# Block 0's matmul operands made one unit earlier, in an unused weight place, the operand steps spread over five units, and the last slot block in another order

## The chip, the cores and the metric

The kernel runs on one core of a Trainium2 chip. The metric is the device time of one execution in microseconds (us), as the median over several executions. The core's engines each work through an instruction list of their own and wait for each other by semaphores: TensorE (PE, matmuls), VectorE (DVE), ScalarE (ACT), GpSimd (POOL), and SyncE (SP), which here only starts transfers (DMAs). ACT starts some transfers too, in the same list as its arithmetic.

## The reference

Three stages follow each other, each on the output of the one before, all in float32:

```python
x = attention(q, k, v, omega)          # random features, 4 x 576 tokens, 8 heads of 64 -> (2304, 512)
# stage 2: 4 experts, all of them on all tokens
for e in range(4):
    h = np.maximum(x @ w1[e], 0.0)     # 512 -> 1024
    out += p[:, e:e + 1] * (h @ w2[e]) # 1024 -> 512, p from domain_probs
# stage 3: 32 slots, 4 for each of 8 experts
logits = x @ phi
d = softmax over the tokens of logits
slot_input = d.T @ x                   # 32 x 512
slot_out = relu(slot_input @ w1[e]) @ w2[e]
return softmax over the slots of logits @ slot_out
```

## The kernel before

**Stage 2, where most of the time goes.** The 2304 tokens are cut into three blocks (0 to 2) and the 4 experts into two halves of their hidden width, so 8 groups. A unit is one group on one block; units 0 to 23 run group by group, so units 0 to 2 are the first group on blocks 0, 1, 2. Every number is split into a high and a low part, and a matmul piece is three matmuls (high by high, high by low, low by high).

**Products.** Units 0 to 2 multiply the plain operands: `plain1` runs eight products of the first matrix (PE, line L558, into the accumulators X and B). From unit 3 on the first matrix is multiplied with seven products (`product1`, also L558) of sums of operand quarters, after the Strassen-Winograd scheme. The second matrix is always done with seven products (`product2`, L765), one unit late, interleaved with the next unit's first-matrix products. Between the two lie the evacuations: relu and split into high and low (ACT L542 and L607 for the high parts such as s3h, DVE L545 and L611 for the low parts such as s3l, s2l, s4l), DVE L671, L703 and L625 for sums, ACT L635 to L639 for copies of X into u, and L812/L814 for copies v of the second matrix's result, which DVE adds up at L808 and scales into the output x at L745 and L747.

**Operands.** What units 3 and up multiply has to be made from each block's plain operand first. This is done once for each block b, in steps: W, `whole` (DVE: high plus low into one float32 array, for each of 4 quarters `KH[0..3]`; L489, for block 0 L492 with the low parts from a transfer), T, `block_sum` (DVE L497, 4 differences of quarters, in place), S, `block_split` (for each of 4 results I4 to I7: ACT L508 casts the high part into `xh`, DVE L510 subtracts it, and two ticks later two transfers from ACT's list, L513 and L514, store both to `xt` in DRAM, from which later units load them). `xh` has two places. Which step runs at which place of which unit is a table of numbers in `prep_steps`, keyed (unit, step): an even step 2i follows first-matrix product i, an odd one 2i + 1 second-matrix product i.

**Block 0's source.** Its quarters come back from DRAM (`xd`, written at L282) by eight transfers on SP's list (`fetch`, L469 and L470, high parts into `xr`, low parts into `xl`).

**Slots.** The slot stage takes the finished tokens in blocks b of up to 4 tiles of 128: `slot_turn` (transposes tpm, L983, and ACT copies x2t, L984), `slot_logits` (lq, L992), `slot_sum` (lt, L1003, DVE maximum L1011, ACT exp L1015), `slot_back` (transposes dp, L1044), `slot_gather` (acc, L1062, and its DVE update L1068). Most of these run as tasks in the last units. The last block, of 2 tiles, and what is left of the one before run in an order written out at the end of the stage, up to the first matmul of the slot experts (hq, L1202):

```python
slot_logits(n)
slot_back(n - 1)
keep_warm(4)
slot_sum(n)
slot_gather(n - 1)
keep_warm(6)
keep_warm(10)
slot_back(n)
keep_warm(3)
```

`keep_warm(k)` puts k matmuls (L78, named warm) whose result nobody reads.

Of the kernel before, what the change touches and what calls it, by code (L numbers as in the profile page):

```python
# [9 lines left out]
F32 = mybir.dt.float32  # L10
# [6 lines left out]
P = 128  # L17
# [28 lines left out]
def body(ctx: ExitStack, tc: tile.TileContext, ql, kl, vl, om, dp, wl, phi, w2l, out):  # L46
# [376 lines left out]
    def weight_split(which, G, i):  # L423
        src = stage[which, G][i]
        p, s = (w1p, w1s) if which == "w1" else (w2p, w2s)
        hi = p.tile([P, 2, HD], F32R, name=f"{which}h", tag=f"{which}h{i}")
        lo = p.tile([P, 2, HD], F32R, name=f"{which}l", tag=f"{which}l{i}")
        nc.scalar.copy(out=hi, in_=src)  # L428
        nc.gpsimd.tensor_tensor(out=lo, in0=src, in1=f32(hi), op=ALU.subtract)  # L429
        s[G, i] = hi, lo  # L430
# [31 lines left out]
    lows = {}  # L462

    def fetch():
        t = x2p.tile([P, 4, 2 * TH], F32, name="xl", tag="x2_1")
        for n, (k, half) in enumerate(KH):
            place(0, (k, half))
            src = xd[0][half][:, k]
            nc.sync.dma_start(out=three(blocks[0, (k, half)]), in_=f32(src[:, 0]))  # L469
            nc.sync.dma_start(out=three(t[:, n]), in_=f32(src[:, 1]))  # L470
            lows[k, half] = t[:, n]

    def place(b, kh):
        k, half = kh
# [42 lines left out]

    def prep_steps():
        W, T, S = whole, block_sum, block_split
        unit1 = [  # L520
            (W, 1, KH[0]), (W, 0, KH[0]), (W, 1, KH[1]), (W, 0, KH[1]), (W, 0, KH[2]), (W, 0, KH[3]), (T, 0, 0),
            (T, 0, 1), (W, 1, KH[2]), (T, 0, 2), (W, 1, KH[3]), (T, 0, 3), (S, 0, I5), (S, 0, I4),
        ]
        unit2 = [
            (T, 1, 0), (T, 1, 1), (S, 0, I6), (S, 0, I7), (W, 2, KH[0]), (W, 2, KH[1]), (T, 1, 2), (T, 1, 3),
            (S, 1, I6), (S, 1, I4), (W, 2, KH[2]), None, (W, 2, KH[3]), (S, 1, I5), (S, 1, I7),
        ]
        unit3 = [
            None, None, *((T, 2, n) for n in range(4)), (S, 2, I6), (S, 2, I5), None, None, None,
            (S, 2, I7), (S, 2, I4),  # L530
        ]
        return {(u + 1, n): f for u, l in enumerate((unit1, unit2, unit3)) for n, f in enumerate(l) if f}
# [431 lines left out]
    def slot_tasks(b):  # L964
# [178 lines left out]
    tp = bank("bq", "tps")[:, 0:NK * NS].rearrange("p (k s) -> p k s", k=NK)  # L1143
    for m, (lhs, rhs) in enumerate(((mo(0), sf), (s2, sumr[0:64, 0, :]))):
        for k in range(NK):
            nc.tensor.matmul(
                tp[:, k, :], lhsT=lhs[:, k * P:(k + 1) * P], rhs=rhs,
                start=m == 0 and k == 0, stop=m == 1, skip_group_check=True,
            )
# [220 lines left out]
```

## Time and profile before

| | |
|---|---|
| median of 3 runs (lowest, highest) | 985.41 us (984.46, 985.44) |
| the profiled execution, its span | 985.5 us, 983.6 us |
| instructions | 18106 |
| busy: PE, DVE, ACT, POOL | 950.3 us (97%), 700.5 us (71%), 501.3 us (51%), 344.0 us (35%) |
| mean granted TensorE clock | 0.993 of full speed |

The span is the stretch from the first to the last recorded instruction of the profiled execution. PE is busy nearly all of it, so a change can shorten the time in three ways: less PE work, less PE waiting (in all some 30 us), or PE running at full clock where it did not.

### The profile page before, as it was taken

To read this page: it belongs to the slowest core of one execution; us is meant where nothing else is said; L and a number is where in the kernel's file an instruction comes from. 1 tells how busy PE (TensorE), PEld (TensorE's weight loads), DVE (VectorE), ACT (ScalarE), POOL (GpSimd) and SP (SyncE) were. 2 spreads that over 40 slices of the span, in tenths; PEclk is the share of its full clock that TensorE was granted. 3 is DMA by queue.
4 is the path that set the end of the run, shared out by engine and by line. 5 is a ranking of instruction groups with operands and counts; after the bars stand their busy time and mean duration, and the time that the engine had idled before them with its cause. 6 is when DMAs were issued, how large, how long until landed. Compare 5 with 4: busy or idle time off the path is not lost.

```text
span 983.6 us, 18106 instructions
## 1 busy us (share of the span) xinstructions
PE 950.3 (97%) x7084; PEld 907.2 (92%) x7084; DVE 700.5 (71%) x1268; ACT 501.3 (51%) x940; POOL 344.0 (35%) x288
## 2 busy tenths in 40 slices
PE   8999999998899999999999999999999999998897
PEld 8999989998799999999999999999999999796644
DVE  6888874797887666886676876666876667757332
ACT  5899885444454444545355444435454444535322
POOL 7878872242343241433134232505332341000000
PEclk9999999998999999999999999999999999999999
DMA  8578754845796665776757566665756564447996
GB/s 281 185 252 292 238 192 150 320 145 195 273 308 230 200 225 185 269 269 230 236 189 225 182 229 221 206 211 195 230 191 235 185 220 162 135 156 299 401 419 271
DMA packets 63220, 227.18 MB, mean 231 GB/s; under 512 B 8352, under 2 KB 17696, under 8 KB 59040
## 3 DMA queue, kind: packets, MB, share of 16 engines
q1 hardware_dynamic: 59392, 215.81, 63.9%
q10 hardware_dynamic: 3744, 10.23, 2.6%
q8 instruction: 56, 0.92, 0.4%
q14 instruction: 28, 0.23, 0.1%
HBM read 202.42 MB, written 23.59 MB: 230 GB/s over the span
## 4 chain that ended last, share of the span: by engine, by line
PE 85%; DVE 8%; ACT 3%; DMA 2%; issue 1%; SPq 1%; ACTq 0%; DVEq 0%
PE X L558 19%; PE X L765 17%; PE B L558 14%; PE B L765 12%; PE kv L220 3%; PE num L244 3%; PE Xq L765 2%; PE pj L176 2%; PE so L1230 2%; PE pj L177 2%; PE pj L178 2%; PE tp L234 2%; PE Bq L765 1%; PE hq L1202 1%; DMA xl<-xd 1%
## 5 line engine op out<-in xcount | busy, mean ns | idle before, releaser
L558 PE MATMUL X<-x,w1h 128*128 128x384 f32 x768 | 196.5, 336 | 2.2 <-ACT u L637 2.2
L558 PE MATMUL B<-x,w1h 128*128 128x384 f32 x600 | 153.3, 336 | 3.0 <-issue 2.6
L558 PEld LDWEIGHTS X<-x,w1h 128*128 128x128 f32 x768 | 134.4, 189 | 4.3 <-ACT u L637 2.4
L558 PE MATMUL X<-x,w1l 128*128 128x384 f32 x384 | 128.5, 335 | 0.0
L415 POOL TENSOR_TENSOR Tw<-raww 128x512 f32<-128x512 f32 x30 | 44.2, 1494 | 195.1 <-DMA raww<-wl 195.1
L558 PEld LDWEIGHTS B<-x,w1h 128*128 128x128 f32 x600 | 104.8, 189 | 3.4 <-issue 2.7
L558 PE MATMUL B<-x,w1l 128*128 128x384 f32 x300 | 100.4, 335 | 0.0
L625 DVE TENSOR_TENSOR u<-B,u 128x768 f32<-128x768 f32 x23 | 22.0, 957 | 98.6 <-PE B L558 98.6
L201 ACT ACTIVATE fe<-pj,nb 128x128 f32<-128x128 f32 x288 | 82.8, 390 | 10.1 <-DVE nb L194 9.3
L558 PEld LDWEIGHTS X<-x,w1l 128*128 128x128 f32 x384 | 72.2, 188 | 0.0
L429 POOL TENSOR_TENSOR w1l<-Tw,w1h 128x512 fp32r<-128x512 f32 x28 | 37.5, 1340 | 94.2 <-ACT w1h L428 94.2
L429 POOL TENSOR_TENSOR w2l<-raww,w2h 128x512 fp32r<-128x512 f32 x24 | 32.4, 1349 | 84.5 <-ACT w2h L428 76.7
L184 DVE TENSOR_REDUCE stat<-pj 128x4 f32<-128x512 f32 x72 | 49.5, 687 | 10.1 <-PE pj L178 9.2
L558 PEld LDWEIGHTS B<-x,w1l 128*128 128x128 f32 x300 | 56.3, 188 | 0.0
L429 POOL TENSOR_TENSOR w2l<-Tw,w2h 128x512 fp32r<-128x512 f32 x32 | 42.5, 1330 | 38.3 <-ACT w2h L428 38.3
L151 POOL TENSOR_TENSOR lo<-raw,hi 128x512 fp32r<-128x512 f32 x35 | 44.7, 1277 | 20.8 <-ACT hi L148 20.2
L429 POOL TENSOR_TENSOR w1l<-raww,w1h 128x512 fp32r<-128x512 f32 x25 | 38.6, 1544 | 37.2 <-ACT w1h L428 37.2
L607 ACT CAST s3h<-X 128x768 fp32r<-128x768 f32 x21 | 16.8, 801 | 65.7 <-DVE X L545 65.7
L176 PE MATMUL pj<-om_hi,hi 128*128 128x256 f32 x144 | 45.1, 313 | 2.1 <-ACT fe L201 1.1
L747 DVE SCALAR_TENSOR_TENSOR x<-B,pr,x 128x256 f32<-128x256 f32 x108 | 45.6, 477 | 1.3
L812 ACT COPY v<-X 128x768 f32<-128x768 f32 x42 | 33.7, 801 | 21.2 <-PE X L765 21.1
L178 PE MATMUL pj<-om_hi,lo 128*128 128x256 f32 x144 | 40.7, 283 | 1.0 <-POOL lo L151 0.8
(294 smaller groups left out, 3042.0 us busy)
## 6 DMA issues: line engine op xcount, KB each, us to landing
x<-xt SPq DMA_DIRECT2D x84, 768.0 KB, 4.3
x<-xd SPq DMA_DIRECT2D x75, 768.0 KB, 4.5
raww<-wl SPq DMA_DIRECT2D x16, 1024.0 KB, 7.2
w2tb<-w2l SPq DMA_DIRECT2D x11, 1024.0 KB, 13.4
raw<-ql SPq DMA_DIRECT2D x18, 512.0 KB, 4.3
xd<-xst SPq DMA_DIRECT2D x36, 256.0 KB, 2.7
raw<-kl SPq DMA_DIRECT2D x16, 512.0 KB, 4.5
w2ta<-w2l SPq DMA_DIRECT2D x5, 1024.0 KB, 6.9
```

The lines of the kernel that those rows point to most:

```text
L151: (nc.gpsimd if i else nc.vector).tensor_tensor(out=lo, in0=r, in1=f32(hi), op=ALU.subtract)
L176: nc.tensor.matmul(o, lhsT=hi[:, pi, :], rhs=om_hi, start=True, stop=False)
L178: nc.tensor.matmul(o, lhsT=lo[:, pi, :], rhs=om_hi, start=False, stop=True)
L184: nc.vector.tensor_reduce(out=stats(i)[:, 4 * g:4 * g + 4, 0], in_=pjs[i, g], axis=AX.X, op=ALU.max)
L201: nc.scalar.activation(out=feats[i][:, 4 * g + h, :], in_=pjs[i, g][:, h, :], func=AF.Exp, bias=biases[i, g][:, h:h + 1], scale=1.0,)
L220: nc.tensor.matmul(kvps[b][h // 4][:, h % 4, :], lhsT=feats[i][p0:p0 + np_, h, :], rhs=v[p0:p0 + np_, h, :], start=first and h % 4 == 0, s ...
L415: nc.gpsimd.tensor_tensor(out=out_, in0=a, in1=b_, op=op)
L429: nc.gpsimd.tensor_tensor(out=lo, in0=src, in1=f32(hi), op=ALU.subtract)
L558: nc.tensor.matmul(o, lhsT=lhs[:, jp, c], rhs=rhs[:, :, k, :], start=first and not k and not n, stop=False, skip_group_check=True,)
L747: nc.vector.scalar_tensor_tensor(out=o, in0=src, scalar=w, in1=o, op0=ALU.mult, op1=ALU.add)
L765: nc.tensor.matmul(q[:, n, :], lhsT=lhs[:, jp, p, :], rhs=rhs[:, jp, :], start=i in (I1, I2, I7) and n % 2 == 0 and jp == 0 and m == 0, st ...
L812: nc.scalar.copy(out=v("v1"), in_=q)
```

## The change

It has five parts.

1. Block 0's four whole quarters lie in a new tile `whole0`, whose place (tag `w1x`) later holds the split weights of the three products I5, I7 and I3, which the plain first group doesn't use. The low parts of block 0 go to places of split operands (I5, I6, I3, I4) that are not yet in use. From group 1 on the weights of I5, I7 and I3 share one tile instead of having six.
2. `fetch` is called one unit earlier, at the last but one attention tile, so its eight transfers stand among the stores of L282 on SP's list.
3. The table in `prep_steps` is another. DVE steps by unit: before 0, 14, 14, 8, 0 in units 0 to 4, after 8, 12, 8, 6, 2. The total is the same (36).
4. Among the slot tasks only block 0 keeps the empty place between back and gather, so block 1's gather and all tasks behind it come one place earlier.
5. The last slot block is in another order, `slot_gather` is split in two (matmuls, then DVE's update), `sf` is computed earlier, the warm matmuls have a bank of their own, and there are 9 instead of 23 of them.

```diff
+    spare = [w1p.tile([P, 4, 2 * TH], F32, name="whole0", tag="w1x")]
...
-        hi = p.tile([P, 2, HD], F32R, name=f"{which}h", tag=f"{which}h{i}")
-        lo = p.tile([P, 2, HD], F32R, name=f"{which}l", tag=f"{which}l{i}")
+        if which == "w1" and i in (I5, I7, I3):
+            if len(spare) == 1:
+                spare.append(w1p.tile([P, 3, 2, 2, HD], F32R, name="w1x", tag="w1x"))
+            hi, lo = (spare[1][:, (I5, I7, I3).index(i), l] for l in range(2))
+        else:
+            hi = p.tile([P, 2, HD], F32R, name=f"{which}h", tag=f"{which}h{i}")
+            lo = p.tile([P, 2, HD], F32R, name=f"{which}l", tag=f"{which}l{i}")
...
-        t = x2p.tile([P, 4, 2 * TH], F32, name="xl", tag="x2_1")
-        for n, (k, half) in enumerate(KH):
-            place(0, (k, half))
+        for n, (kh, i) in enumerate(zip(KH, (I5, I6, I3, I4))):
+            k, half = kh
+            blocks[0, kh] = spare[0][:, n]
+            lows[kh] = htile(i, 1, F32)
...
+        return {
+            (0, 6): [(W, 0, KH[0])],
+            (0, 8): [(W, 0, KH[1])],
...
+            (2, 11): [(S, 1, I7)],
+            (2, 12): [(S, 1, I4)],
+            (3, 1): [(T, 2, 0)],
+            (3, 3): [(T, 2, 1)],
...
+            (4, 3): [(S, 2, I4)],
+        }
...
+        if i == n_seq - 2:
+            fetch()
...
-    fetch()
...
+            wait = [[]] if b == 0 else []
+            tasks = [turns[0:2], turns[2:], [], [logits], [total], [], [back], *wait, [gather], [share1], [share2]]
...
     slot_turn(n, 1, 2, 4)
+    slot_back(n - 1)
     slot_turn(n, 1, 0, 2)
+    acc = slot_gather1(n - 1)
     slot_logits(n)
-    slot_back(n - 1)
-    keep_warm(4)
+    slot_gather2(n - 1, acc)
+    keep_warm(2, "qx")
     slot_sum(n)
-    slot_gather(n - 1)
-    keep_warm(6)
-    keep_warm(10)
+    keep_warm(7, "qx")
+    sf = mp.tile([P, NS], F32, name="sf")
+    nc.vector.tensor_scalar_mul(sf, sumr[:, 0, :], st["f", n])
     slot_back(n)
-    keep_warm(3)
...
+    slots_turn(0, mo(0), sf)
     acc = bank("aq", "acc")[0:64, :]
...
-    sf = mp.tile([P, NS], F32, name="sf")
-    nc.vector.tensor_scalar_mul(sf, sumr[:, 0, :], st["f", n])
...
+    slots_turn(1, s2, sumr[0:64, 0, :])
```

Line numbers of the changed kernel are 7 to 39 higher than before: L489, L497, L508, L510, L513, L514, L545 and L814 become L496, L504, L515, L517, L520, L521, L573 and L842.

ACT's list in unit 2, before, from the copy v of a second-matrix product (v_3330) to the one behind it (v_3432); xr_2944 holds half of block 0, xt_2 and xt_4 two of its results in DRAM:

```order
L812 COPY v_3330<-X_3311 128x768
L607 CAST e22h<-u_3186 128x768
L508 CAST xh<-xr_2944 128x768
L428 CAST w1h<-Tw_3148 128x512
L542 ACTIVATE e11h<-X_3288 128x768
L542 ACTIVATE u_3352<-X_3288 128x768
L508 CAST xh<-xr_2944 128x768
L513 DMA xt_2_104<-xh 128x768
L514 DMA xt_2_104<-xr_2944 128x768
L428 CAST w1h<-Tw_3148 128x512
L513 DMA xt_4_106<-xh 128x768
L514 DMA xt_4_106<-xr_2944 128x768
L814 COPY v_3432<-X_3311 128x768
```

The same place of the changed kernel; xt_2_108 belongs to block 1:

```order
L840 COPY v_3343<-X_3324 128x768
L635 CAST e22h<-u_3124 128x768
L435 CAST w1x<-Tw_3170 128x512
L570 ACTIVATE e11h<-X_3303 128x768
L570 ACTIVATE u_3363<-X_3303 128x768
L435 CAST w1x<-Tw_3170 128x512
L842 COPY v_3432<-X_3324 128x768
L515 CAST xh<-xr 128x768 x2
L520 DMA xt_2_108<-xh 128x768
L521 DMA xt_2_108<-xr 128x768
L570 ACTIVATE e12h<-B_3397 128x768
```

Block 0's two casts and four stores no longer stand ahead of the second copy v; the first stores of block 1 stand behind it.

DVE's list around the start of unit 3, before (s, B, u: intermediate sums of unit 2's result, of which the parts s3l, s2l, s1l, s4l are split off; xr_3538 and xr_3404: block 2):

```order
L808 TENSOR_TENSOR B_3499<-B_3499,v_3432 128x768
L745 TENSOR_SCALAR x_1_3310<-B_3499,pr 128x256 x3
L510 TENSOR_TENSOR xr<-xr,xh 128x768 x2
L545 SCALAR_TENSOR_TENSOR s_3630<-B_3569,u_3540 128x768
L545 SCALAR_TENSOR_TENSOR B_3569<-B_3569,u_3352 128x2x384
L671 TENSOR_TENSOR s_3631<-s_3630,u_3352 128x768
L611 TENSOR_TENSOR s3l<-B_3569,s3h 128x768
L703 TENSOR_TENSOR u_3452<-u_3452,s_3631 128x768
L611 TENSOR_TENSOR s2l<-s_3631,s2h 128x768
L611 TENSOR_TENSOR s1l<-s_3630,s1h 128x768
L625 TENSOR_TENSOR B_3702<-B_3702,u_3666 128x2x384
L497 TENSOR_TENSOR xr_3404<-xr_3538,xr_3404 128x768
```

And in the changed kernel:

```order
L517 TENSOR_TENSOR xr<-xr,xh 128x768 x2
L836 TENSOR_TENSOR B_3504<-B_3504,v_3432 128x768
L773 TENSOR_SCALAR x_1_3323<-B_3504,pr 128x256 x3
L573 SCALAR_TENSOR_TENSOR s_3631<-B_3570,u_3540 128x768
L573 SCALAR_TENSOR_TENSOR B_3570<-B_3570,u_3363 128x2x384
L699 TENSOR_TENSOR s_3632<-s_3631,u_3363 128x768
L639 TENSOR_TENSOR s3l<-B_3570,s3h 128x768
L731 TENSOR_TENSOR u_3455<-u_3455,s_3632 128x768
L639 TENSOR_TENSOR s2l<-s_3632,s2h 128x768
L504 TENSOR_TENSOR xr_3345<-xr_3498,xr_3345 128x768
L639 TENSOR_TENSOR s1l<-s_3631,s1h 128x768
L653 TENSOR_TENSOR B_3700<-B_3700,u_3665 128x2x384
```

The two splits (L510, now L517) stand ahead of the sum of B and v instead of directly ahead of s, and the first difference of block 2 (L497, now L504) has moved from behind L625 to ahead of s1l.

PE's list at the end of the slot stage, before:

```order
L983 MATMUL tpm<-ident,x_2_3676 128x128 x8
L992 MATMUL lq<-x2t,phis 32x256 x4
L1044 MATMUL dp<-ident,mo 128x64 x4
L78 MATMUL warm<-om_hi 128x256 x4
L1003 MATMUL lt<-mo,sumr 128x256
L1062 MATMUL acc<-x_2_3676,d 32x512 x4
L78 MATMUL warm<-om_hi 128x256 x16
L1044 MATMUL dp<-ident,mo 128x32 x2
L78 MATMUL warm<-om_hi 128x256 x3
L1135 MATMUL acc<-x_2_3676,d 32x512 x2
L1146 MATMUL tps<-sf,mo 128x32 x4
```

And in the changed kernel:

```order
L1013 MATMUL tpm<-ident,x_2_3673 128x128 x6
L1074 MATMUL dp<-ident,mo 128x64 x4
L1013 MATMUL tpm<-ident,x_2_3673 128x128 x2
L1092 MATMUL acc<-x_2_3673,d 32x512 x4
L1022 MATMUL lq<-x2t,phis 32x256 x4
L78 MATMUL warm<-om_hi 128x256 x2
L1033 MATMUL lt<-mo,sumr 128x256
L78 MATMUL warm<-om_hi 128x256 x7
L1074 MATMUL dp<-ident,mo 128x32 x2
L1174 MATMUL tps<-sf,mo 128x32 x4
L1182 MATMUL acc<-x_2_3673,d 32x512 x2
```

The block before the last is turned back and gathered (dp, acc) ahead of lq, and the last block's first tps group runs ahead of its acc.

## Rows read from the trace of the kernel before

**Rows 1.** PE's waits by releaser: us in total, times, longest.

```profile
PE X L765 <- ACT v L814: 4.5, 1, 4.5
PE B L558 <- issue: 2.6, 1, 2.6
PE X L558 <- ACT u L637: 2.2, 1, 2.2
...
PE X L765 <- DVE s2l L611: 0.8, 1, 0.8
...
PE B L558 <- DVE s3l L611: 0.5, 1, 0.5
```

**Rows 2.** Timeline of DVE, unit 1: start, us, work, idle before and its releaser.

```profile
185.76 0.96 DVE L492 TENSOR_TENSOR xr<-xr,xl 128x768 f32<-128x768 f32 x1 [3.19 <-DMA xl<-xd]
```

**Rows 3.** Timeline of ACT, unit 2 (ACTq is ACT's transfer list).

```profile
226.97 0.33 ACTq L514 DMA_DIRECT2D xt<-xr  x1
227.34 0.80 ACT L814 COPY v<-X 128x768 f32<-128x768 f32 x1 [3.29 <-DVE xr L510]
```

**Rows 4.** Timeline of DVE, units 2 and 3.

```profile
245.41 0.97 DVE L808 TENSOR_TENSOR B<-B,v 128x768 f32<-128x768 f32 x1 [2.10 <-PE B L765]
...
247.60 2.92 DVE L510 TENSOR_TENSOR xr<-xr,xh 128x768 fp32r<-128x768 f32 x2
...
257.55 1.16 DVE L497 TENSOR_TENSOR xr<-xr,xr 128x768 f32<-128x768 f32 x1
259.23 0.96 DVE L545 SCALAR_TENSOR_TENSOR e11l<-B,e11h 128x768 fp32r<-128x768 f32 x1 [0.52 <-ACT u L542]
```

**Rows 5.** Timeline of ACT, unit 3.

```profile
264.27 0.80 ACT L637 COPY u<-X 128x768 f32<-128x768 f32 x1 [5.08 <-DVE s4l L611]
```

**Rows 6.** Windows: PE, PEld, DVE, ACT, POOL busy, granted clock, DMA share, GB/s.

```profile
170.00:180.00 10.00, 10.00 (x66) 9.96 (x66) 5.46 (x7) 5.24 (x9) 2.58 (x3) 1.00 0.62 181
...
228.00:232.00 4.00, 3.81 (x18) 3.81 (x19) 4.00 (x5) 1.55 (x3) 0.00 (x0) 0.50 0.75 246
```

**Rows 7.** The chain that ended last, unit 2: start, us, what.

```profile
228.19 4.21 PE X L765 x18
...
234.76 2.15 PE B L765 x18
```

**Rows 8.** Timeline of DVE, unit 1, a W step.

```profile
204.01 2.05 DVE L489 TENSOR_TENSOR xr<-x 128x768 f32<-128x768 f32 x1
```

**Rows 9.** Timeline of POOL, the same time.

```profile
203.14 2.09 POOL L415 TENSOR_TENSOR Tw<-raww,Tw 128x512 f32<-128x512 f32 x1
```

**Rows 10.** Timeline of PE, end of the slot stage.

```profile
918.20 0.28 PE L765 MATMUL Bq<-w2h,e22l 128*128 128x256 f32 x1
...
921.63 0.64 PE L992 MATMUL lq<-x2t,phis 128*32 128x256 f32 x8 [1.53 <-ACT x2t L984]
...
922.77 1.22 PE L78 MATMUL warm<-om_hi 128*128 128x256 f32 x4
923.79 1.05 PE L1003 MATMUL lt<-mo,sumr 128*128 128x256 f32 x2
...
927.16 2.16 PE L78 MATMUL warm<-om_hi 128*128 128x256 f32 x16 [0.88 <-DVE mo L1068]
929.26 0.31 PE L1044 MATMUL dp<-ident,mo 32*128 32x32 f32 x2
929.49 0.63 PE L78 MATMUL warm<-om_hi 128*128 128x256 f32 x3
...
933.47 1.92 PE L1202 MATMUL hq<-pre,sp 128*32 128x512 f32 x16
```

**Rows 11.** Timeline of ACT, the last block's exp.

```profile
926.04 0.19 ACT L1015 ACTIVATION_READ_ACCUMULATOR mo<-lt,mrun 128x1 f32 x1
```

**Rows 12.** Timeline of DVE, the copy of the last acc.

```profile
931.55 0.42 DVE L1142 COPY mo<-acc 64x256 f32<-64x256 f32 x1 [1.58 <-ACT mo L1141]
```

**Rows 13.** Windows around the end of the slot stage, columns as in rows 6.

```profile
921.00:924.00 3.00, 2.37 (x17) 1.84 (x18) 0.91 (x3) 0.58 (x3) 1.55 (x2) 0.72 1.01 423
```

More of the change, by code (lines that the diff above doesn't have):

```diff
@@ L464, in fetch @@
     def fetch():
-        t = x2p.tile([P, 4, 2 * TH], F32, name="xl", tag="x2_1")
-        for n, (k, half) in enumerate(KH):
-            place(0, (k, half))
+        for n, (kh, i) in enumerate(zip(KH, (I5, I6, I3, I4))):
+            k, half = kh
+            blocks[0, kh] = spare[0][:, n]
+            lows[kh] = htile(i, 1, F32)
             src = xd[0][half][:, k]
-            nc.sync.dma_start(out=three(blocks[0, (k, half)]), in_=f32(src[:, 0]))
-            nc.sync.dma_start(out=three(t[:, n]), in_=f32(src[:, 1]))
-            lows[k, half] = t[:, n]
+            nc.sync.dma_start(out=three(blocks[0, kh]), in_=f32(src[:, 0]))
+            nc.sync.dma_start(out=three(lows[kh]), in_=f32(src[:, 1]))
     def place(b, kh):
@@ L519, in prep_steps @@
         W, T, S = whole, block_sum, block_split
[L520 to L532, printed above, removed]
+        return {
+            (0, 6): [(W, 0, KH[0])],
+            (0, 8): [(W, 0, KH[1])],
+            (0, 10): [(W, 0, KH[2]), (W, 0, KH[3])],
+            (0, 12): [(T, 0, 0), (T, 0, 1)],
+            (0, 14): [(T, 0, 2), (T, 0, 3)],
+            (1, 0): [(S, 0, I6)],
+            (1, 1): [(S, 0, I5)],
+            (1, 2): [(W, 1, KH[0])],
+            (1, 4): [(W, 1, KH[1])],
+            (1, 5): [(S, 0, I7)],
+            (1, 6): [(S, 0, I4)],
+            (1, 7): [(W, 1, KH[2])],
+            (1, 9): [(W, 1, KH[3])],
+            (1, 10): [(T, 1, 0)],
+            (1, 11): [(T, 1, 1)],
+            (1, 12): [(T, 1, 2)],
+            (1, 13): [(T, 1, 3)],
+            (2, 1): [(W, 2, KH[0])],
+            (2, 3): [(W, 2, KH[1])],
+            (2, 5): [(S, 1, I6)],
+            (2, 6): [(S, 1, I5)],
+            (2, 8): [(W, 2, KH[2])],
+            (2, 10): [(W, 2, KH[3])],
+            (2, 11): [(S, 1, I7)],
+            (2, 12): [(S, 1, I4)],
+            (3, 1): [(T, 2, 0)],
+            (3, 3): [(T, 2, 1)],
+            (3, 5): [(T, 2, 2)],
+            (3, 7): [(T, 2, 3)],
+            (3, 9): [(S, 2, I6)],
+            (3, 10): [(S, 2, I5)],
+            (4, 2): [(S, 2, I7)],
+            (4, 3): [(S, 2, I4)],
+        }
     steps = prep_steps()
     def prep_one(u, n):
-        if (u, n) in steps:
-            f, *a = steps.pop((u, n))
+        for f, *a in steps.pop((u, n), ()):
             f(*a)
@@ L969, in slot_tasks @@
         if b < NB - 3:
-            tasks = [turns[0:2], turns[2:], [], [logits], [total], [], [back], [], [gather], [share1], [share2]]
+            wait = [[]] if b == 0 else []
+            tasks = [turns[0:2], turns[2:], [], [logits], [total], [], [back], *wait, [gather], [share1], [share2]]
         elif b == NB - 3:
@@ L1056, in slot_back, with slot_gather1 @@
             st["rest"] = lambda: (back(1, 2), logits())
-    def slot_gather(b):
+    def slot_gather1(b):
         acc = bank("s", "acc")
@@ L1064, in slot_gather, with slot_gather2 @@
             )
+        return acc
+    def slot_gather2(b, acc):
         if b == 0:
@@ L1071, in slot_gather @@
         slot_total(b)
+    def slot_gather(b):
+        slot_gather2(b, slot_gather1(b))
     def slot_share1(b):
@@ L1121, in body, with slots_turn @@
     slot_turn(n, 1, 2, 4)
+    slot_back(n - 1)
     slot_turn(n, 1, 0, 2)
+    acc = slot_gather1(n - 1)
     slot_logits(n)
-    slot_back(n - 1)
-    keep_warm(4)
+    slot_gather2(n - 1, acc)
+    keep_warm(2, "qx")
     slot_sum(n)
-    slot_gather(n - 1)
-    keep_warm(6)
-    keep_warm(10)
+    keep_warm(7, "qx")
+    sf = mp.tile([P, NS], F32, name="sf")
+    nc.vector.tensor_scalar_mul(sf, sumr[:, 0, :], st["f", n])
     slot_back(n)
-    keep_warm(3)
+    tp = bank("bq", "tps")[:, 0:NK * NS].rearrange("p (k s) -> p k s", k=NK)
+    def slots_turn(m, lhs, rhs):
+        for k in range(NK):
+            nc.tensor.matmul(
+                tp[:, k, :], lhsT=lhs[:, k * P:(k + 1) * P], rhs=rhs,
+                start=m == 0 and k == 0, stop=m == 1, skip_group_check=True,
+            )
+    slots_turn(0, mo(0), sf)
     acc = bank("aq", "acc")[0:64, :]
@@ L1142, in body @@
     nc.vector.tensor_copy(out=s2[:, HD:DM], in_=acc[:, HD:DM])
[L1143 to L1149, printed above, removed]
+    slots_turn(1, s2, sumr[0:64, 0, :])
     st["rest"]()
```

## The prediction

> **What bounds the kernel now.** I read the page first, then PE's waits, the windows and the chain around the longest of them, and then DVE's and ACT's timelines there. PE is busy 97% of the span, and the change gives it no other matmuls to do but for 14 warm ones fewer. So the question is which of PE's waits go, which come, and where its clock is below full. PE's waits by releaser [rows 1] show five that belong to the units in which operands are made: 4.5 us for ACT's copy v, 2.6 us put down to "issue", 2.2 us for ACT's copy u, 0.8 and 0.5 us for s2l and s3l, together 10.6 us. The reader is to see that each stands there once, in a kernel that has 24 such units: they belong to units 2 and 3, not to the steady state. The second place is the end of the slot stage, where PE works through small dependent pieces [rows 10].
>
> **The first two waits (0.8 and 0.5 us, start of unit 2).** DVE makes s, s3l and s2l of unit 1's result, and it comes late because 14 operand steps are in unit 1's list, and because it waited 3.19 us for block 0's low parts to land [rows 2]. Afterwards unit 1 has 12 steps: two at 0.96 us (the W step of rows 2) are 1.9 us less, and the wait for the transfer leaves unit 1, since `fetch` is issued a unit ahead. Together 5.1 us less ahead of a lateness of 1.3 us. Gain 1.3 us, bounds 0 and 1.3.
>
> **The third wait (4.5 us, unit 2).** The copy v stands in ACT's list behind the store of block 0's split; that store started at 226.97, v at 227.34, after ACT had waited 3.29 us for DVE's L510 [rows 3]. So it is the order of ACT's list, not v itself, that held PE. In the changed list the stores of block 0 are gone from there, and block 1's first two stores stand behind v. DVE, whose L510 was the last cause, has 8 steps in unit 2 instead of 14. Gain 4.5 us, bounds 0 and 4.5.
>
> **The fourth and fifth waits (2.6 and 2.2 us, unit 3).** "issue" names no releaser. DVE's timeline does: it stood idle 2.10 us ahead of L808, then did two L510 (2.92 us) before it could begin s [rows 4], and s3l, for which PE waited, comes after s. In the changed list the two splits stand ahead of L808, where DVE was idle, and six other steps have left unit 2. So s begins about 2.9 us earlier, more than the 2.6 us of the wait: it goes. PE then asks 2.6 us earlier for the copy u, which waits for s4l [rows 5]. The rows from s to s4l are as many as before, so s4l comes 2.9 us earlier by the shift, but one T step (L497) has moved from behind L625 to ahead of s1l. There it cost little before: it lay beside ACT's work, after which DVE was still idle for 0.52 us [rows 4]. Ahead of s1l it delays all that follows by about 0.9 us. The rest of this wait is then 2.2 + 2.6 - 2.9 + 0.9 = 2.8 us. POOL's four sums (L415) come again in unit 3, and a step of DVE that meets one can take twice its time: 2.05 us for a W step beside a POOL sum of 2.09 us [rows 8, 9], against 0.96 in rows 2, so 1.1 us more. Whether one meets T or s4l depends on when a weight transfer lands, which the trace of before does not decide; I take half, so 3.3 us, bounds 2.8 and 4.8 (all of it stays). Gain 4.8 - 3.3 = 1.5 us, bounds 0 and 2.0.
>
> [...]
>
> **The clock.** [...] Gain 2.1 us, bounds 0 (it falls in unit 3 instead) and 2.1.
>
> **Unit 0 and the earlier transfers.** Unit 0 gets 8 DVE steps, 8 x 0.96 = 7.7 us. They lie beside PE's products: DVE was busy 5.46 of 10 us from 170 to 180 [rows 6], so some 4.5 us in each 10 are free, three times over in a unit of 32 us. The last four (T) stand ahead of unit 0's evacuations; without that cover they would cost up to 3.8 us at the start of unit 1. The eight transfers of block 0 move past stores of L282 on SP's list, which must wait for the last attention tiles; nothing on PE waits for those stores there, and the DMA share at that end is 0.62 [rows 6]. I book nothing. The third product's weights share one tile now; their casts and sums wait for the same matmuls as before, piece by piece. Units 3 and 4 get the last two splits later (2 steps in unit 4), where xt of block 2 is first loaded for unit 5, a unit later. Nothing.
>
> **The end of the slot stage.** It runs from the last L765 of the last unit (918.20 + 0.28 = 918.48) to hq (933.47), 15.0 us [rows 10]. Of that: lq starts after 3.15, lt after 5.31, exp's sum is done at 926.04 + 0.19 = 926.23, after 7.75 [rows 11], but the last dp, which needs no more than exp, starts only after 10.78. It stands behind 16 warm matmuls, which themselves waited 0.88 us for DVE's L1068 (they share a bank with acc). New order: lq's own wait of 1.53 us was for ACT, so the dp and acc put ahead of it lie in waits, and lq stays at 3.15. Between lq and lt go the dp (922.77 - 921.63 - 0.64 = 0.5 us) and half of the four warm ones (0.5 us): lt after 4.3. Exp's sum comes 2.44 us after lt as before: 6.7, and dp follows at once. From dp to hq it was 4.2 us; the three warm ones (0.6) go, but the last copy of acc [rows 12], which ran beside the first tps group, now stands open, two halves of 0.4 us: 4.4 us. hq after 11.1 us, a gain of 3.9 us. Bounds: 2.5, if lq is held back by the acc ahead of it and lt by DVE's L1068, which now stands ahead of the copy of lq; and 4.5, if the open copy costs nothing. The tasks of block 1 one place earlier shift small waits in the last units; no row prices them, and I book nothing, bounds -0.5 and +0.8.
>
> **Sum.** 1.3 + 4.5 + 1.5 + 2.1 + 3.9 = 13.3 us. The profiled execution took 985.5 us, the same as the median of the runs (985.41) within 0.1, so 985.5 - 13.3 = 972.2 us.
>
> **The rivals.**
> 1. *DVE and POOL collide* in units 1 and 3. For it: the W step of 2.05 us [rows 8, 9]. Against it: the steps are fewer in unit 1. Then the first two waits come back (1.3), the one in unit 3 is 4.8 (1.5), and the clock falls after it (2.1): 977.1 us.
> 2. *The wait in unit 2 moves, it doesn't go.* Block 1's stores stand ahead of e12h in ACT's list, and they too wait for an L517 of DVE. If DVE comes to it as late as before [rows 3], PE waits for e12h as it did for v: the 4.5 and the 2.1 us stay, 978.8 us. Against it: six steps fewer on DVE in unit 2.
> 3. *The clock falls at the end of the slot stage.* The granted clock there was 0.72 from 921 to 924 already [rows 13], with 23 warm matmuls; with 9 the end may fall to half once more and lose what rows 7 show for one fall, 2.1 us: 974.3 us. [...]
> 4. *Slower:* the splits wait for their stores. `xh` has two places, and the spread table puts W or T between splits, so that each third cast waits until a store has landed. If DVE's L517 then stands idle ahead of PE's evacuations at each of the five changes of pair, by as much as PE waited for a store ahead of v (4.5 us, rows 1), that is 22.5 us: 994.7 us. It decides the sign (13.3 + 2.0 us) from 3.4 such waits in full. Against it: a store is due within one or two products, and the new table leaves three and more between pairs.
> 5. *Nothing changes:* the total of DVE's steps is the same, 36, and the waits only move to unit 1: about 985 us.
>
> **How the numbers follow.** Forecast 0.60; rivals 1 to 3: 0.12, 0.10, 0.12; rival 4: 0.03; rival 5: 0.03. The time is the forecast's, 972.2. Its own range is 969.0 to 975.5: below by the upper bounds (0.5 in unit 3, 0.6 at the end, 0.8 for the tasks make 970.3, and 1.3 more for what I can't price), above by the lower bounds of the end (1.4) and of unit 3 (1.5), 975.1. The whole range reaches on to rival 2: 969.0 to 979.0. Outside lie rivals 4 and 5 and a tenth of the forecast. 0.2% is 2.0 us, about what a measurement of this kernel can tell from no change. Faster: 0.60 + 0.12 + 0.10 + 0.12 = 0.94; same 0.03; slower 0.03.
>
> **What would show it.** In the new trace PE's waits should show no row for v over 0.5 us, none for s3l and s2l, no "issue" of 2.6, and one row of 2.5 to 4 us for the copy u of unit 3, released by s4l. The granted clock should be 1.00 in unit 2. From the last L765 to hq it should be about 11 us, with dp right behind exp. DVE's wait for the low parts should be gone. I am wrong if DVE's list in unit 1 is still full at its end, if e12h is the new wait in unit 2, or if the windows of units 2 and 3 or of the end still show 0.50.

## The result and the profile after

The changed kernel took 979.14 us (median of 6 executions), the kernel before 985.99 us beside it on the same chip (6 executions). The ratio is 0.9911 with a 95% interval of 0.9883 to 0.9939: faster by 0.9%, where 1.4% (13.3 us) had been forecast. One execution of the six took 4645 us and is left out of the ratio. The other five lie at 974.8 to 979.5 us, with a mean granted clock of 0.996 in the shorter and 0.991 in the longer ones. The profiled one took 978.94 us, its span is 977.1 us, 6.5 less than before.

How the lead over the kernel before grows and shrinks is seen when the same matmul is looked up in both traces (start in us; 0.2 us of the lead are there from the start of the units):

| place | before | after | lead |
|---|---|---|---|
| unit 2, third X product | 228.19 | 221.22 | 7.0 |
| unit 2, the B product behind it | 234.60 | 225.46 | 9.1 |
| unit 3, first B product behind s3l | 254.24 | 242.38 | 11.9 |
| unit 3, behind the copy u | 269.46 | 261.73 | 7.7 |
| unit 4, behind the copy v | 299.10 | 292.52 | 6.6 |
| last unit, before the slot tasks | 888.43 | 881.85 | 6.6 |
| end of the last L765 (now L793) | 918.48 | 913.47 | 5.0 |
| start of hq | 933.47 | 924.79 | 8.7 |
| end of the span | 983.62 | 977.13 | 6.5 |

So 11.9 us, nearly all that the early part had to give, were won by unit 3, and 5.4 us of them were lost again further on. The end of the slot stage won 3.7 us and gave back 2.2 behind hq.

PE's waits by releaser (us in total, times, longest), which answer to [rows 1]:

```profile
PE X L586 <- ACT u L665: 4.0, 1, 4.0
...
PE lq L1022 <- ACT x2t L1014: 2.5, 3, 1.3
...
PE X L793 <- ACT v L842: 0.9, 1, 0.9
```

The rows for s2l, s3l and "issue" are gone. The row for v fell from 4.5 to 0.9 us and is another one: it stands in unit 4, not in unit 2. The row for the copy u has grown from 2.2 to 4.0 us and is now the longest wait of the whole execution.

DVE's, POOL's and ACT's timelines around it (start, us, work, idle before and its releaser), which answer to [rows 4, 5]:

```profile
251.13 1.01 DVE L504 TENSOR_TENSOR xr<-xr 128x768 f32<-128x768 f32 x1
252.07 2.01 DVE L639 TENSOR_TENSOR s4l<-u,s4h 128x768 fp32r<-128x768 f32 x1
```

```profile
248.78 2.55 POOL L417 TENSOR_TENSOR Tw<-raww 128x512 f32<-128x512 f32 x2 [8.61 <-DMA raww<-wl]
251.29 3.91 POOL L417 TENSOR_TENSOR Tw<-raww,Tw 128x512 f32<-128x512 f32 x2
```

```profile
254.19 0.80 ACT L665 COPY u<-X 128x768 f32<-128x768 f32 x1 [6.14 <-DVE s4l L639]
```

The split s4l took 2.01 us while POOL did its sums from 251.29 on, and ACT's copy u stood behind it. Before, POOL's four sums were over at 262.48, ahead of s4l:

```profile
263.22 0.94 DVE L611 TENSOR_TENSOR s4l<-u,s4h 128x768 fp32r<-128x768 f32 x1
```

What the clock did behind this wait, and behind the end of the slot stage (windows: PE, PEld, DVE, ACT, POOL busy, granted clock, DMA share, GB/s; answering to [rows 6, 13]):

```profile
252.00:254.00 2.00, 0.00 (x0) 0.00 (x0) 2.00 (x2) 0.00 (x0) 1.92 (x2) 0.85 0.28 117
254.00:256.00 2.00, 0.96 (x3) 0.96 (x4) 2.00 (x3) 1.50 (x2) 1.20 (x1) 0.50 0.00 0
256.00:258.00 2.00, 2.00 (x8) 2.00 (x7) 1.75 (x3) 0.00 (x0) 0.00 (x0) 0.50 0.00 0
258.00:260.00 2.00, 2.00 (x9) 2.00 (x9) 0.00 (x0) 0.67 (x1) 0.00 (x0) 0.50 0.00 0
...
918.00:921.00 3.00, 2.31 (x18) 1.94 (x16) 1.20 (x6) 1.11 (x4) 0.95 (x2) 1.00 1.02 431
921.00:924.00 3.00, 2.53 (x12) 1.62 (x12) 0.42 (x1) 0.37 (x1) 0.00 (x0) 0.74 1.01 421
924.00:927.00 3.00, 3.00 (x17) 1.18 (x20) 1.63 (x9) 0.58 (x2) 0.00 (x0) 0.50 1.00 418
927.00:930.00 3.00, 3.00 (x20) 0.71 (x16) 2.21 (x10) 0.48 (x2) 0.00 (x0) 0.62 1.02 426
```

Half speed (granted 0.50) from about 254 to 260 us, and again from about 922 to 929 (0.74, 0.50 and 0.62 in the last three windows), right where hq runs. The price of the first stands in the chain that ended last (start, us, what), which answers to [rows 7]:

```profile
255.04 4.21 PE X L586 x12
259.25 2.64 PE X L793 x18
```

At full clock 12 matmuls of L558 take 2.08 us and 18 of L765 2.15 us, together 4.2. Here the first starts at 255.04 and the product behind both at 261.73 (the table above), 6.7 us later, so 2.5 us were lost to the clock. The second fall cost 2.2 us: from hq's start to the end of the span it is 52.3 us, before it was 50.2.

The new wait for v, in unit 4, on ACT's and DVE's timelines:

```profile
289.05 0.33 ACTq L521 DMA_DIRECT2D xt<-xr  x1
289.41 0.80 ACT L842 COPY v<-X 128x768 f32<-128x768 f32 x1 [3.07 <-PE X L586]
```

```profile
286.88 1.27 DVE L775 SCALAR_TENSOR_TENSOR x<-B,pr,x 128x256 f32<-128x256 f32 x3
288.06 0.95 DVE L517 TENSOR_TENSOR xr<-xr,xh 128x768 fp32r<-128x768 f32 x1
```

It is the picture of [rows 3] once more: the copy v (289.41) stands in ACT's list behind a store (L521, 289.05), the store waits for DVE's split L517 (done at 289.01), and the split stands in DVE's list behind the sums of the unit. The releaser that the row of v names (PE) is the one that came last by semaphores; what held it is the store ahead of it. Here it is the second of block 2's two splits that were moved to unit 4. (The PE product named in the row ends at 289.38, the store at the same time, so this trace alone can't tell them apart; e7 does, where the store stands elsewhere and the wait is gone.)

The end of the slot stage on PE's timeline, answering to [rows 10]:

```profile
913.19 0.28 PE L793 MATMUL Bq<-w2h,e22l 128*128 128x256 f32 x1
...
916.31 0.62 PE L1022 MATMUL lq<-x2t,phis 128*32 128x256 f32 x8
916.86 0.51 PE L78 MATMUL warm<-om_hi 128*128 128x256 f32 x2
917.48 0.70 PE L1033 MATMUL lt<-mo,sumr 128*128 128x256 f32 x2
...
919.54 0.31 PE L1074 MATMUL dp<-ident,mo 32*128 32x32 f32 x2 [0.54 <-ACT mo L1045]
920.00 1.08 PE L1174 MATMUL tps<-sf,mo 128*128 128x32 f32 x8 [0.15 <-DVE sf L1168]
921.01 1.05 PE L1182 MATMUL acc<-x,d 128*32 128x512 f32 x4
922.53 1.91 PE L1174 MATMUL tps<-sumr,mo 64*128 64x32 f32 x8 [0.47 <-ACT mo L1186]
```

From 913.47 on: lq after 2.8 us, lt after 4.0, dp after 6.1, hq after 11.3 (before 3.15, 5.3, 10.8, 15.0). The second tps group takes 1.91 us, the first 1.08: the clock has fallen between them (granted 1.00 from 920 to 922, 0.61 from 922 to 924).

### The profile page after: what moved, and what is told of

It reads as the page before. It is cut to its first block, busy times and chain, and to the rows that moved or that the text cites. A ratio compares the mean times of both kernels' runs of the same rounds, so it can differ in the third digit from the quotient of the medians.

```text
span 977.1 us, 18078 instructions
## 1 busy us (share of the span) xinstructions
PE 950.0 (97%) x7070; PEld 906.3 (93%) x7070; DVE 697.4 (71%) x1268; ACT 501.4 (51%) x940; POOL 346.3 (35%) x288
## 4 chain that ended last, share of the span: by engine, by line
PE 89%; DVE 5%; ACT 3%; DMA 1%; issue 1%; SPq 0%; ACTq 0%; DVEq 0%
PE X L586 20%; PE X L793 18%; PE B L586 15%; PE B L793 13%; PE kv L220 3%; PE num L244 3%; PE Xq L793 2%; PE pj L176 2%; PE hq L1241 2%; PE so L1269 2%; PE Bq L793 1%; PE pj L177 1%; PE pj L178 1%; PE tp L234 1%; DMA raw<-kl 1%; PE tpx L265 1%
## 5 line engine op out<-in xcount | busy, mean ns | idle before, releaser
L586 PE MATMUL X<-x,w1h 128*128 128x384 f32 x432 | 110.4, 336 | 0.1
L586 PE MATMUL B<-x,w1h 128*128 128x384 f32 x432 | 110.2, 336 | 0.0
L586 PE MATMUL X<-x,w1x 128*128 128x384 f32 x504 | 96.6, 340 | 4.0 <-ACT u L665 4.0
L586 PEld LDWEIGHTS X<-x,w1x 128*128 128x128 f32 x504 | 87.6, 192 | 5.9 <-ACT u L665 4.2
L586 PEld LDWEIGHTS X<-x,w1h 128*128 128x128 f32 x432 | 75.5, 189 | 0.2 <-PE Xq L793 0.2
L586 PEld LDWEIGHTS B<-x,w1h 128*128 128x128 f32 x432 | 75.5, 189 | 0.0
L586 PE MATMUL B<-x,w1l 128*128 128x384 f32 x216 | 72.3, 335 | 0.0
L586 PE MATMUL X<-x,w1l 128*128 128x384 f32 x216 | 72.3, 335 | 0.0
L586 PE MATMUL B<-x,w1x 128*128 128x384 f32 x252 | 47.4, 336 | 0.0
L436 POOL TENSOR_TENSOR w1x<-Tw,w1x 128x512 fp32r<-128x512 f32 x21 | 28.4, 1356 | 52.4 <-ACT w1x L435 52.4
```

The costliest lines, as they stand in the source:

```text
L586: nc.tensor.matmul(o, lhsT=lhs[:, jp, c], rhs=rhs[:, :, k, :], start=first and not k and not n, stop=False, skip_group_check=True,)
```

## The experiments

Each kernel was run beside the kernel before on one chip, which took a median of 987.9 us beside e1 to e4, 987.0 beside e5 to e8 and 986.5 beside e9 and e10; the ratios are to that.

**e1: the operand part alone.** The slot tasks and the last slot block are put back:

```diff
-            wait = [[]] if b == 0 else []
-            tasks = [turns[0:2], turns[2:], [], [logits], [total], [], [back], *wait, [gather], [share1], [share2]]
+            tasks = [turns[0:2], turns[2:], [], [logits], [total], [], [back], [], [gather], [share1], [share2]]
...
-    acc = slot_gather1(n - 1)
     slot_logits(n)
-    slot_gather2(n - 1, acc)
-    keep_warm(2, "qx")
+    slot_back(n - 1)
+    keep_warm(4)
...
```

> Parts 1 to 3 of the change alone; the slot tasks and the last slot block are as before. My theory, from the two traces: the operand part gains 9.1 us up to the middle of unit 2 and 2.7 us at the start of unit 3, gives 4.2 us back in unit 3 (the copy u waits 4.0 us for s4l, and the clock falls behind it) and 1.1 us in unit 4: net 6.6 us, so 979 us, with the end of the slot stage as in rows 10 (15.0 us from the last L765 to hq). Rival: the two halves of the change are not independent, and the operand part alone gives the whole 6.5 us only with the new end: then this kernel is at 981 us or more.

Measured: 978.34 us (976.66 to 979.37), ratio 0.9911 (0.9888 to 0.9935), the same as the whole change. The lead is 11.8 us at the start of unit 3, 8.3 behind the copy u (which PE waited for 4.4 us), 7.2 from unit 5 to the end of the last L765: my theory's course, with 0.6 us less lost in unit 3. So the operand part carries the whole gain. From the last L765 to hq it was 13.45 us, not 15.0 as expected: here the clock stayed at 1.00 through the old end, where the kernel before had 0.72 [rows 13].

**e2: the slot part alone.** The kernel before with the new task list and the new last slot block.

> Parts 4 and 5 alone, operands as before. My theory: the end of the slot stage gains 3.7 us (11.3 instead of 15.0 us), the tasks one place earlier lose about 1.5 us, and the clock at half speed behind the end loses 2.2 us: net 0, 985.5 us, with a granted clock of about 0.5 right behind hq's start. Rival: the clock's fall behind the end hangs on the new early part (other time of the fall), not on the end itself; then the clock holds and this kernel is at 983 us.

Measured: 986.88 us (984.76 to 990.57), ratio 0.9999 (0.9983 to 1.0015). By time the net is nothing, as the theory had it. "T to hq", the time from the end of the last L765 to hq's start, took 10.6 us, and around hq's start the clock fell:

```profile
925.00:929.00 4.00, 3.31 (x23) 2.28 (x21) 1.40 (x6) 1.11 (x4) 1.16 (x2) 1.00 1.01 424
929.00:933.00 4.00, 3.53 (x20) 1.77 (x22) 1.59 (x8) 0.94 (x3) 0.00 (x0) 0.69 1.01 420
933.00:937.00 4.00, 4.00 (x40) 1.16 (x36) 2.99 (x14) 0.96 (x3) 0.00 (x0) 0.88 1.02 424
```

hq starts at 931.31, in the stretch of 0.69. The rival, that the clock would hold with the old early part, is out. The lead of this kernel is -0.6 us ahead of the last unit's tasks and -2.2 at the end of the last L765: the tasks one place earlier cost 1.6 us. So the slot part by itself is -1.6, +4.4 up to hq and -1.2 behind it, 1.5 us won in this profile against a profile of before whose old end had lost 1.5 us to the clock. The -0.6 ahead of it is the untouched early part: the clock fell in unit 3 of this execution,

```profile
266.00:268.00 2.00, 2.00 (x8) 2.00 (x8) 0.00 (x0) 0.08 (x1) 0.00 (x0) 0.50 0.00 0
```

behind the second of the same two waits as in the kernel before (2.5 and 2.8 us here, 2.6 and 2.2 there). Behind the first it stood at 1.00 up to 264 us, and in the profile of before it stands at 1.00 behind both.

**e3: two differences behind s4l.**

```diff
-            (3, 1): [(T, 2, 0)],
-            (3, 3): [(T, 2, 1)],
+            (3, 4): [(T, 2, 0), (T, 2, 1)],
```

> The changed kernel with one edit: the first two differences of block 2 are made behind s4l in unit 3 instead of ahead of it. My theory: they are what s4l is late by, so the wait for the copy u falls from 4.0 to about 2.2 us, the clock holds behind it as it did behind 2.6 us before, and the time is 1.8 + 2.6 us less: 974.5 us. Rival: POOL's sums decide; s4l then meets an earlier one and stays as late, the wait stays near 4 us, the clock falls, 978.5 us.

Measured: 973.5 us (971.78 to 974.48), ratio 0.9860 (0.9837 to 0.9884). The wait for u fell further than expected, to 1.2 us, since s4l now began at 250.01 instead of 252.07 and took 0.95 us instead of 2.01:

```profile
250.01 0.95 DVE L638 TENSOR_TENSOR s4l<-u,s4h 128x768 fp32r<-128x768 f32 x1
250.88 2.02 DVE L504 TENSOR_TENSOR xr<-xr,xr 128x768 f32<-128x768 f32 x1
```

The step behind it took the 2.02 us, and nobody waits for that one. The clock behind the wait:

```profile
252.00:254.00 2.00, 2.00 (x12) 2.00 (x13) 1.97 (x2) 0.57 (x1) 2.00 (x2) 1.00 0.20 83
```

The lead behind the copy u is 13.2 us instead of 7.7. The rival did not come in this profile: s4l took 0.95 us. In e7, with the differences in the same place, s4l did meet a sum and took 1.98 us, and the wait was 2.3 us.

**e4: the old places of the tasks.**

```diff
-            wait = [[]] if b == 0 else []
+            wait = [[]]
```

> The changed kernel with part 4 undone: block 1 keeps the empty place between back and gather. My theory: the tasks one place earlier cost about 1.5 us in the last units (the lead of the changed kernel falls there from 6.6 to 5.0 us), so 977.4 us. Rival: those waits are the same work seen elsewhere and come back later, 978.9 us.

Measured: 978.02 us (977.17 to 978.63), ratio 0.9907 (0.9886 to 0.9928). By time alone it can't be told from the changed kernel, since the wait for u was longer in this profile (5.0 us). The trace tells it: the lead is 6.1 us in unit 5 and still 6.1 at the end of the last L765, where the changed kernel falls from 6.6 to 5.0. T to hq is 11.9 us instead of 11.3, so 0.5 of the 1.6 us come back there. A net cost of about 1 us for part 4, by one profile.

**e5: a store ahead of v in unit 2 again.**

```diff
-            (2, 3): [(W, 2, KH[1])],
-            (2, 5): [(S, 1, I6)],
-            (2, 6): [(S, 1, I5)],
+            (2, 3): [(S, 1, I6)],
+            (2, 4): [(S, 1, I5)],
+            (2, 6): [(W, 2, KH[1])],
```

> The changed kernel with block 1's first two splits three places earlier in unit 2, so that a store of block 1 stands ahead of the copy v in ACT's list, as block 0's stores did before; one W step of block 2 goes behind them. My theory: a wait of PE for v comes back in unit 2, since the store waits for DVE's L517; how long it is hangs on how late DVE comes to it, and DVE has 8 steps there instead of 14, so 1 to 3 us instead of 4.5: 980 to 982 us. Rival: DVE's load alone made the wait, and the place of the store is harmless now: no wait for v in unit 2, 979 us.

Measured: 977.52 us (976.93 to 980.32), ratio 0.9905 (0.9884 to 0.9926). The wait came back, but with 0.9 us, less than I had expected:

```profile
PE X L793 <- ACT v L842: 1.8, 2, 0.9
```

Two waits of 0.9 us now, one in unit 2 at 221.3 and the one in unit 4. On ACT's timeline the store (L521) starts at 220.98 and v at 221.35; DVE's L517, for which the store waited, ended at 220.95, behind the sums of the unit. So the place of the store makes the wait, against the rival. That DVE's load makes its size is argued from two kernels only: 0.9 us with 8 steps in the unit, 4.5 with 14. The difference in time is below what the runs can tell.

**e6: more warm matmuls in the waits of the end.**

```diff
-    keep_warm(7, "qx")
+    keep_warm(12, "qx")
...
+    keep_warm(5, "qx")
     slots_turn(1, s2, sumr[0:64, 0, :])
```

> The changed kernel with 10 more warm matmuls at the end of the slot stage, where PE waits anyway: 12 instead of 7 ahead of the last dp, and 5 new ones ahead of the second tps group. They cover 0.54 and 0.47 us of waits. My theory: it is PE's idle and thin stretch ahead of hq that lets the clock fall, so it holds: hq to the end takes 50.1 us instead of 52.3, T to hq stays at 11.3, 2 us less than the changed kernel, 977 us where the clock falls in unit 3. Rival: matmuls of that kind don't keep the clock, or the fall was set off earlier: hq to the end stays at 52.3 us.

Measured: 975.39 us (975.16 to 977.65), ratio 0.9885 (0.9863 to 0.9907). The windows at the end, against those of the changed kernel above:

```profile
918.00:921.00 3.00, 2.85 (x20) 1.71 (x19) 0.41 (x2) 1.02 (x4) 0.00 (x0) 1.00 0.98 410
921.00:924.00 3.00, 2.88 (x25) 2.10 (x27) 1.21 (x6) 0.63 (x2) 0.00 (x0) 1.00 1.02 426
924.00:927.00 3.00, 3.00 (x32) 0.91 (x28) 2.05 (x9) 0.62 (x2) 0.00 (x0) 1.00 1.04 434
```

Full clock throughout. hq to the end 50.2 us instead of 52.3, and T to hq 10.8 instead of 11.3, with the clock at 1.00 from 921 to 924 where the changed kernel has 0.74: 2.7 us for ten matmuls that nobody reads. The other kernels bear it out: in e8 and e10, which have the same ten, hq to the end takes 50.1 us too; in the seven profiles with the new end without them (the changed kernel, e2 to e5, e7, e9) it takes 51.4 to 52.6, and the clock falls there each time. In unit 3 nearly the same wait, 4.1 us, cost less clock than in the changed kernel (lead 8.8 behind it instead of 7.7), because full speed came back earlier:

```profile
258.00:260.00 2.00, 2.00 (x17) 2.00 (x17) 0.00 (x0) 1.24 (x2) 0.00 (x0) 1.00 0.28 31
```

In the changed kernel this stretch still shows 0.50.

**e7: block 2's last splits later, on top of e3.**

```diff
-            (4, 2): [(S, 2, I7)],
-            (4, 3): [(S, 2, I4)],
+            (4, 6): [(S, 2, I7)],
+            (4, 8): [(S, 2, I4)],
```

> As e3_t_late, and block 2's last two splits moved from products 1 and 2 of unit 4 to its steps 6 and 8. My theory: PE's wait for v in unit 4 (1.2 us in e3_t_late) is the same mechanism as the one in unit 2 before: a store ahead of v in ACT's list, which waits for a split that DVE does late. With the splits behind that v it goes: 972.3 us. Rival: the store delays another evacuation instead (the copy u or e12h, behind which it now stands), or a load of unit 5 waits for it, and the time stays at 973.5 us.

Measured: 972.64 us (970.36 to 975.15), ratio 0.9850 (0.9826 to 0.9874). There is no wait for v left, and none took its place: the lead stays at 11.35 us from unit 3 to unit 6. In the same profile s4l met a POOL sum again and the wait for u was 2.3 us, but the clock held behind it.

**e8: all edits that should help together** (e3, e4, e6 and e7):

> All edits that should help together: differences behind s4l (e3), late splits (e7), the old places of the tasks (e4), and the warm matmuls (e6). My theory: 973.5 less 1.2 for v, 0.9 for the places and 2.2 for the clock behind hq: 969.2 us. Rival: with the old places the end waits longer for the block before the last (T to hq was 11.9 instead of 11.3 us in e4), and the warm matmuls lie on the path: 971 us or more.

Measured: 970.0 us (969.68 to 970.28), ratio 0.9823 (0.9807 to 0.9839), 0.8 us above the expectation. PE's waits in the places of the change:

```profile
PE X L585 <- ACT u L664: 2.2, 1, 2.2
PE lq L1021 <- ACT x2t L1013: 2.0, 3, 0.8
```

The rival's part is there too: T to hq is 11.5 us, of which one wait of 1.0 us for the block before the last. The mean granted clock is 0.999 in each of the runs, and they lie within 0.6 us, those of the changed kernel within 4.7.

**e9: the weights of POOL's sums loaded two products later,** as a test of the collision, on the changed kernel:

```diff
-        if b == 2 and G < LAST and i == (I4 if u > 2 else 7):
+        if u == 3 and i == I2:
+            raw_load("w2", 1)
+        if b == 2 and 0 < G < LAST and i == I4:
             raw_load("w2", G + 1)
```

> The changed kernel with one load moved: the raw second-matrix weights of group 1 are loaded two products later in unit 3, so that POOL's four sums of them begin after s4l and not before it. T's place is left as it is. My theory: the wait for the copy u is made of two parts, T ahead of s4l and s4l beside a POOL sum (2.0 instead of 0.95 us); without the second the wait falls from 4.0 to about 2.9 us, and s4l takes 0.95 us. If the clock holds behind 2.9 us the time falls by 3.5 us, if not by 1.1. Rival: the longer duration of s4l has another cause (a late operand), it stays at 2 us and the wait at 4 us.

Measured: 976.14 us (973.47 to 977.31), ratio 0.9885 (0.9863 to 0.9908). DVE's and POOL's timelines:

```profile
252.90 0.95 DVE L504 TENSOR_TENSOR xr<-xr 128x768 f32<-128x768 f32 x1
253.76 0.95 DVE L639 TENSOR_TENSOR s4l<-u,s4h 128x768 fp32r<-128x768 f32 x1
```

```profile
254.63 5.09 POOL L417 TENSOR_TENSOR Tw<-raww 128x512 f32<-128x512 f32 x2 [12.69 <-DMA raww<-wl]
```

POOL began at 254.63, just behind s4l, which took 0.95 us; the wait was 2.9 us, as expected, and the window behind it:

```profile
256.00:258.00 2.00, 2.00 (x14) 2.00 (x13) 1.32 (x2) 0.33 (x1) 2.00 (x1) 1.00 0.01 3
```

The clock held. Behind it 1.1 us went again in small waits, 0.4 of them ahead of unit 4's first product, the place that e10 shows. The rival (another cause for the 2 us) is out.

**e10: the same load later on top of e8.**

> As e8_all_edits, and the same load two products later. My theory: the wait for the copy u in unit 3 (2.2 us in e8_all_edits) falls to about 1.2 us, 969.0 us. Rival: the sums then come too late for the second-matrix weights of unit 4 and PE waits there by as much or more: 970 us or above.

Measured: 971.8 us (971.37 to 973.16), ratio 0.9851 (0.9831 to 0.9870), 1.8 us more than e8, though the two intervals overlap a little. The wait for u fell to 1.2 us as expected, but the rival's time came:

```profile
271.26 0.59 PE L585 MATMUL X<-x,w1h 128*128 128x384 f32 x2 [1.70 <-issue]
```

A new wait of 1.7 us ahead of unit 4's first product, and 0.7 us more behind it. The row names no releaser, but DVE's and POOL's timelines do. In e10:

```profile
262.20 3.76 DVE L774 TENSOR_SCALAR x<-v,pr 128x256 f32<-128x256 f32 x3
...
270.22 0.95 DVE L638 TENSOR_TENSOR s3l<-X,s3h 128x768 fp32r<-128x768 f32 x1
```

```profile
260.65 2.55 POOL L436 TENSOR_TENSOR w2l<-raww,w2h 128x512 fp32r<-128x512 f32 x2
263.15 2.65 POOL L436 TENSOR_TENSOR w2l<-Tw,w2h 128x512 fp32r<-128x512 f32 x2
```

And in e8:

```profile
262.94 0.97 DVE L772 TENSOR_SCALAR x<-v,pr 128x256 f32<-128x256 f32 x3
...
268.17 0.95 DVE L638 TENSOR_TENSOR s3l<-X,s3h 128x768 fp32r<-128x768 f32 x1
```

The product writes the accumulator X, of which there is one, and s3l still reads it: s3l ends at 271.17, and PE starts at 271.26. DVE comes to s3l 2.1 us later than in e8, since its three steps on v took 3.76 us beside POOL's late work instead of 0.97. So these 1.7 us were no wait for the weights, which the rival had named; the collision with POOL moved to another step of DVE.

## Why the prediction was off by half

The direction and most mechanisms were right, the size was not: 13.3 us were forecast, 6.5 came in the profiled execution, 0.9% of the time by the ratio instead of 1.4%. Step by step:

- *First two waits:* 1.3 us forecast. They are gone, and so is DVE's wait for the low parts; the lead grew by 2.0 us there. Right, though 0.6 us of it shows in e2 as well, where this part is the old one.
- *Third wait with its clock:* 4.5 + 2.1 us forecast (the 2.1 is the difference of the two times in [rows 7]), 6.9 measured. Right, and e5 shows that a store in that place makes such a wait (0.9 us there).
- *Fourth wait:* it was to go, 2.6 us. It went, 2.7 us.
- *Fifth wait: here the prediction failed.* I worked out 2.8 us without a collision with POOL and 3.9 with one, and took half, 3.3, which no execution could be. The measured 4.0 is the case with a collision; e9, without it, gave the 2.9 of the first. In e4 both T and s4l met a sum (1.97 and 2.01 us), a case that I had not counted, and the wait was 5.0. The term was mis-sized by 0.7 us, towards what rival 1 had said of unit 3.
- *The clock behind it:* this was the costlier half of the same step. I took the clock to hold behind the 3.3 us that I left there. That was an estimate between two waits of the trace of before, of 2.6 us, behind which it held (1.00 from 254 to 258 us), and of 4.5 us, behind which it fell [rows 6]. With 4.0 us the clock fell, 2.5 us. The runs draw no sharp line: behind the 2.9 us of e9 it held, behind the 2.8 of e2, shortly after another wait of 2.5, it fell. One profile can't price the clock near this length; I should have kept both cases open with half the chance each.
- *Unit 4:* "nothing", I wrote, looking only at when block 2's results are loaded, not at what stands behind their stores in ACT's list. It cost 1.2 us. It is rival 2's mechanism, and I had looked for it in unit 2 alone. e7 removes it.
- *The tasks one place earlier:* booked at nothing, bounds -0.5 to +0.8, measured -1.6 (the same in e2; about -1 net by e4). No row priced it, and the bound was too tight.
- *The end of the slot stage:* 3.9 us forecast, 3.7 measured up to hq. Right in size, but e1 shows that 1.5 of the 15.0 us before were half-speed clock in that one execution, not the order; with full clock on both sides T to hq is 13.5 us (e1) against 10.8 (e6), 2.7 less. And rival 3 came on top: 2.1 us were its price, 2.2 came. With 9 warm matmuls the clock fell in each profile, with 19 it held in all three (e6, e8, e10).

Added up: 2.0 + 6.9 + 2.7 - 4.2 (fifth wait and clock, lead 11.9 to 7.7) - 1.2 - 1.6 + 3.7 - 2.2 = 6.1 us, with the 0.2 us from the start 6.3 of the span's 6.5. The likeliest case did not come; rival 3 and, in unit 3 alone, rival 1 did, together. I had given each a chance of 0.12 by itself and not worked out their sum (972.2 + 1.5 + 2.1 + 2.1 = 977.9 us), though both turn on the same thing, whether the clock holds behind PE's waits. Of the prediction's own signs of being wrong one came: windows of unit 3 and of the end at 0.50. That the 978.9 us of the profiled execution still lie within the range, up to 979.0, is luck: its upper end was rival 2's, whose wait did not come in unit 2. No wait of PE by rival 4 (splits that wait for their stores to land) or 5 was seen.

What stays open: which of the two falls is missing in the shorter executions of the changed kernel (974.8 us at a clock of 0.996). That they differ by a fall of the clock is argued from the granted clocks and from e8, where there is neither a fall nor the spread.

## What to carry to other kernels

When a store is issued from an engine's own list, look at what stands behind it there: here it passed its wait on to the copy v (4.5 us in unit 2 before, 0.9 us in e5), and moving the split that it waits for to unit 4 moved the wait along with it (0.9 us there), until the store stood behind the copy (e7, no wait for v). A wait of PE had two prices here, its own length and the clock behind it: behind the waits of 4 us and more the clock took another 1.4 to 2.5 us, behind those of 2.2 to 2.9 us nothing in six cases of seven (the seventh was 2.8 us long, in e2). Warm matmuls that fill waits were not dead weight: ten of them gave 2.7 us back here, and an order that is shorter without them was no gain that could be measured (e2).

## What the runs showed of the hardware

- DVE steps of 128x768 that read two tiles took 0.95 us in most places and up to 2.05 us where a POOL sum was under way (s4l: 2.01 us in the changed kernel, 1.98 in e7, 0.95 in e3 and e9). Not every step beside a sum took longer: in e3 s4l, from 250.01 on, kept its 0.95 us though POOL's first two sums ran from 248.81 to 252.08, and the step behind it took 2.02 us; in e9 the two steps behind s4l took 0.95 us each beside POOL's first two sums, which took 5.09 us there and 2.55 in the changed kernel. DVE's list is the same in e3 and e7 there, so its order alone did not settle which step took longer. Three DVE steps that scale v took 3.76 us beside POOL in e10, 0.97 in e8.
- The clock fell to 0.50 in or behind waits of 4.0 (the changed kernel), 4.3 (e5), 4.4 (e1), 4.5 (before) and 5.0 us (e4), and held at 1.00 behind 1.2 (e3, e10), 2.2 (before, e8), 2.3 (e7), 2.5 (e2), 2.6 (before) and 2.9 us (e9). Behind one of 2.8 us it fell (e2, 0.50 from 266 to 268). It also fell at the end of the slot stage, where the changed kernel's waits were 0.4, 0.5, 0.2 and 0.5 us long (0.61 from 922 to 924); behind the old end's waits of 0.6 and 1.5 us it fell once (before, 0.58 from 922 to 924) and held once (e1), and behind the 0.9 us that follow them it stood at 1.00 in both. How much a fall costs differs between executions: behind nearly the same wait of 4.0 to 4.1 us, a lead of 4.2 us was lost in one profile and 3.2 in another, where full speed was back by 258 us (e6).
